# Four edits of order and place in a fused convolution and mixture-of-experts kernel: earlier first raw weights, a later softmax in the ramp, one ring for row blocks, another bank for a third tile

## The chip, the cores and the metric

One core of a Trainium2 chip runs the whole kernel. The metric is the device time of one execution in microseconds (us). The kernel before took 1184.83 us (median of three runs, 1182.57 to 1186.95). The execution that was profiled took 1184.11 us, of which 1182.5 us lie between its first and its last instruction; a trace covers that span.

Engines: PE multiplies matrices (PEld is its weight load), DVE and ACT work elementwise, POOL computes some and starts the scatters, SP only starts DMAs. Each runs its own instructions in order and waits on semaphores for the others.

## The reference

```python
# 1: causal convolution over 7 positions with a softmax of the given weights, per head
w = exp(weight_gen - max);  w = w / (sum(w) + 1e-9)            # (8, 2880, 8 heads, 7)
x_unf = x_pad[:, idx]                                          # 7 rows back, D = 192 = 8 heads x 24
out = einsum('bshk,bskhg->bshg', w, x_unf)
# 2: two-level routing of N = 23040 tokens: 4 groups x 4 experts, the best one of each
g_idx = argmax(x @ w_group);  e_idx = argmax(xg @ w_expert[g]) # top 1
h  = maximum(xg @ w1[g, e], 0.0)                               # 192 -> 1024
ye = h @ w2[g, e]                                              # 1024 -> 192
out[tok] = g_w * e_w * ye
```

## The kernel before

**Groups.** The tokens go through the first part in 15 groups of 12 slots x 128 partitions. For a group, `load_group` loads x and the weights `wt`; `softmax` works on `wt` (L268 to L282, DVE, with one exponential on ACT at L271); `conv` makes the seven products with x (L297) and adds them (L315) on DVE, for the first six half groups partly by PE matmuls with the identity (L338); `logits` transposes the result on PE (L395, L396) and multiplies by the routing weights; `ranks` finds each token's expert and its rank there, with two small matmuls (L462, L463) that need the one-hot matrix `oh` (L452). POOL then scatters the rows to DRAM by expert (L506).

**Blocks.** The second part works on blocks of rows of one expert. `ROUNDS` says which blocks may be taken after which group: a `table` made on DVE holds each block's place and expert. The order is 10 single blocks of 128 rows (blocks 0 to 9, "singles", `plain`), then blocks of two tiles (256 rows) from block 10 on, one block of three tiles (61), and in the last round blocks 77 to 86 of three tiles ("wide"; 80 to 86 cut), 87 and 88 of two, 89 to 92 of two cut ones, 93 and 94 single. A block takes 4 units (8 if wide); each unit is one `gemm1` (L939, into `ph`, ACT relu into `hh`) and, two units later, one `gemm2` (L977, or L979 and L980, into `py`). `finish` scales `py` by the gate on ACT (L986, for the later blocks with a DVE step L992) and `send` scatters `y` on POOL (L994).

**Inputs of a block.** `load(n, 0)` loads its rows `xb` (L804); `load(n, 1)` and `load(n, 2)` its first weights: two halves of `wa` straight for a single (L819), or for the others into `raw` buffers (L821, L828, the last piece from `w1lo`), which ACT casts to `wa` (L845, L854) with a DVE subtraction for the low part (L869). `load(n, 3)` loads the second weights (L832). All go through SP in the order in which `ask` and `pump` put them. `ask_x(n + 3)` follows `finish(n)`. In the unit u = 0 of a block, ACT copies the next block's columns (`prep_d`, L894); in u = 1 PE transposes its tiles (`prep_x`, L901 for a single, L912 and L913 into `tpx` otherwise), ACT copies them to `xh` (L919) and DVE makes `xl` (L869).

**Order.** The program is written by a planner: `clk` holds the modelled times of the engines, `fill` takes steps of the front part (`front`, `step`, `beside`) as long as DVE's modelled time is behind that of PE, and `after`, `delay` hold back DVE steps. So a changed cost or condition in one place can move steps elsewhere. `side` holds the next softmax, taken three steps at a time in `beside`.

**Buffers that the change touches.** `xb` stands in three tiles of four places, taken by `n % 3`; a two-tile block takes the half `n // 3 % 2`, a wide one the first three places. A load waits until the block that had those places has been scattered: six blocks back for two tiles, three back for wide ones. PSUM tile `tpx` (pool `ps_x`) has one buffer, and so has `tp` (pool `ps_t`), which the logits and the singles use.

Of the kernel before, what the change touches and what calls it, by code (L numbers as in the profile page):

```python
# [9 lines left out]
F32 = mybir.dt.float32  # L10
# [32 lines left out]
def conv_moe_kernel(ctx: ExitStack, tc: tile.TileContext, x, wgen, w_group, w_expert, w1, w2, out):  # L43
# [5 lines left out]
    P = 128  # L49
# [13 lines left out]
    W = D + 2  # L63
# [8 lines left out]
    ENDS = [r[0] for r in ROUNDS]  # L72
# [6 lines left out]
    FIRST = ENDS[0]  # L79
# [4 lines left out]
    tiles_of = lambda nb: CUT.get(nb, nb)  # L84
# [126 lines left out]
            return tiles[(at[0] if i is None else i) % n]  # L211
        return take

    xbs = [const.tile([P, 4, W], F32, name=f"xb{i}") for i in range(3)]
    new_ix = ring("ix", 3, [P, 1], I32)
    new_xd = ring("xd", 2, [P, 3, 2, HP])
    new_xh = ring("xh", 2, [P, 2, 3 * P], F32R)
# [440 lines left out]
    def front():  # L658
        side = []
        set_up()  # L660
        load_group(1)
        next(slow[0][0])
        yield from softmax(0, 0, SC)
        rest = softmax(0, SC)

        def pace(g):
            return 99 if g <= FIRST else HURRY if g < MAIN + 3 else 8 if g in ENDS else 2

        def beside(g, n):
            rush = g >= FIRST and not grp[FIRST - 1].routed  # L670
            if not rush:
                for q in list(slow):
                    yield from move(slow, q, 2)
            for q in side[:1]:
                if not rush:
                    yield from move(side, q, 3)
            yield from routing(g)

        def routing(g):
            if ranking:  # L680
                yield from move(ranking, ranking[0], pace(g))
            if scoring and (not ranking or g < FIRST):
                yield from move(scoring, scoring[0], pace(g) if scoring[0][2].chunks == 2 or g >= FIRST - 1 else 3)

        def settle(g):
            while not grp[g].routed:
                qs = ranking or scoring
                q = qs[0]
                yield from move(qs, q, 99)
                if qs and qs[0] is q and q[1] is not None:  # L690
                    yield Until(q[1][1]) if q[1][0] == "time" else NEXT

        for g in range(ENDS[-1]):
            o = grp[g]
            o.routed = False
            scoring.append([logits(g, o), None, o])
            for n, c in enumerate(conv(g, o)):
                yield c
                if g == 0 and n < 6:
                    for c in islice(rest, None if n == 5 else 1):  # L700
                        yield c
                if n == (2 if state["slots"] else 0) and 1 <= g < ENDS[-1] - 1:
                    load_group(g + 1)
                if n >= (12 if state["slots"] else 4) and not o.ahead and g + 1 < ENDS[-1] and g != FIRST - 1:
                    o.ahead = True
                    side.append([softmax(g + 1), None])
                yield from beside(g, n)
                if g == FIRST - 1 and n in (7, 8):
                    if n == 7:
                        soft = softmax(FIRST)  # L710
                    yield next(soft)
            if g == FIRST - 1:
                for n, c in enumerate(soft):
                    yield c
                    yield from beside(g, n)
            yield from finish_all(side)
            if g:
                yield from settle(g - 1)
        yield from settle(ENDS[-1] - 1)
# [49 lines left out]
    order = []  # L769
# [11 lines left out]
    def plain(n):  # L781
        return order[n][1] == 1

    def load(n, part):
# [11 lines left out]
        o = visits[n]  # L796
        if part == 0:
            nt = tiles_of(nb)
            h = 0 if nt == 3 else n // 3 % 2 * 2
            o.xb = xbs[n % 3][:, h:h + nt, :]  # L800
            o.tx = arrive[r, nb]
            rv = nc.sync.value_load(tab[q:q + 1, 0:1], min_val=0, max_val=NROW)
            full = nt - (nb in CUT)
# [89 lines left out]
        b.td = run("act", 0.1 + 0.13 * b.nt, b.o.tx)  # L893
        nc.scalar.copy(out=b.xd, in_=b.x[:, :, P:D].unsqueeze(2).broadcast_to([P, b.nt, 2, HP]))  # L894

    def prep_x(b, t0):
        fill(b.o.tx)
        if b.plain:
            tp = ps_t.tile([P, 3, P], F32, name="tp")
# [5 lines left out]
            b.txl = 0.0  # L905
            return
        m = min(2, b.nt - t0)
        tp = ps_x.tile([P, 2, 2, P], F32, name="tpx")[:, :, 0:m]
        tpv = tp.rearrange("p a t q -> p a (t q)")
        for t in reversed(range(m)):  # L910
            lo = max(0, min(t * P, b.n - (t0 + 1) * P))
# [109 lines left out]
    def blocks(n0, n1, paced):  # L1021
# [24 lines left out]
        def ask_w(n):  # L1046
            ask(n, 1)
            ask(n, 2)
# [66 lines left out]
        for i in range(len(units) + LAG):  # L1115
            if i < len(units):
                n, u = units[i]
                last = units_of(n) - 1
                gemm1(cur, u)
                queue.append((cur, u))  # L1120
                nxt_at = i + last + 1 - u
                if nxt_at < len(units):
                    if u == 0:
                        pump(units[nxt_at][0])
                        nxt = block(nxt_at)
                        prep_d(nxt)
                    if u == 1:
                        prep_x(nxt, 0)
                    if u == last // 2 + 1 and nxt.nt > 2:
                        prep_x(nxt, 2)  # L1130
                if u == last and i + 1 < len(units):
                    cur = nxt
            asks = []
# [7 lines left out]
            if i < len(units):  # L1141
                n, at = units[i]
                end = at == last
                if end and n + 3 < n1 and (plain(n + 3) or plain(n + 2)):
                    ask_w(n + 3)
                    if not plain(n + 3):
                        ask_w(n + 4)
                did = 0
                for job in list(jobs):
                    m, part, h = job  # L1150
# [60 lines left out]
```

## Time and profile before

| what | value |
|---|---|
| median of three runs | 1184.83 us |
| profiled execution, its own time | 1184.11 us |
| its span | 1182.5 us |
| PE busy | 1119.3 us (95%) |
| DVE busy | 957.2 us (81%) |
| ACT busy | 644.5 us (55%) |
| POOL busy | 572.4 us (48%) |
| granted PE clock, mean | 0.989 of full |
| DMA | 275.10 MB, mean 233 GB/s |

The first 113 us or so hold only the front part; singles run until about 205 us, two-tile blocks until about 955 us, wide ones until about 1105 us, and the rest to the end. The convolutions end near 870 us.

### The profile page before, as it was taken

The page shows a single profiled execution, that of the slowest core. Times are in us where ns is not written, and L with a number is a line of the kernel's source. Part 1 is how long each engine was busy: PE and PEld are TensorE (multiplying, and loading weights), DVE is VectorE, ACT ScalarE, POOL GpSimd, SP SyncE. Part 2 cuts the span into 40 slices and gives each one's busy share as a digit, 9 for nine tenths or more (in the row PEclk, how much of TensorE's full clock was granted, in tenths as well). Part 3 has the DMA queues.
Part 4 walks back from the last instruction along what each step waited for, and adds up shares of the span by engine and source line. Part 5 has one row for each costly group of instructions (what it writes and reads, how often), then busy time and mean ns, then how long its engine had stood idle before and what let it go on. Part 6 is the DMA issues. An engine that isn't in the chain of part 4 may idle for free. (4 is left out here: it accounts for less than half of the span.)

```text
span 1182.5 us, 24615 instructions
## 1 busy us (share of the span) xinstructions
PE 1119.3 (95%) x8357; PEld 1061.8 (90%) x8357; DVE 957.2 (81%) x1682; ACT 644.5 (55%) x1235; POOL 572.4 (48%) x613
## 2 busy tenths in 40 slices
PE   5787899999999999999999999999999989999998
PEld 2444789999999999999999999999899989999997
DVE  8899897999998999999999999998554756556661
ACT  1341334655556556556555556555556756666562
POOL 7164173847174756565555648373766112222211
PEclk9998999999999999999999999999999999999999
DMA  5798799786878886978787968667789774655562
GB/s 174 215 315 227 244 304 313 236 293 210 282 237 278 265 254 213 303 224 290 222 294 217 305 207 281 197 199 222 233 259 254 220 210 138 176 172 181 154 210 79
DMA packets 84520, 275.10 MB, mean 233 GB/s; under 512 B 15490, under 2 KB 34378, under 8 KB 82592
## 3 DMA queue, kind: packets, MB, share of 16 engines
q1 hardware_dynamic: 64056, 229.77, 62.4%
q0 software_dynamic: 20208, 43.39, 12.0%
q8 instruction: 67, 1.10, 0.4%
q14 instruction: 69, 0.57, 0.2%
q10 hardware_dynamic: 120, 0.28, 0.1%
HBM read 225.83 MB, written 48.42 MB: 232 GB/s over the span
## 5 line engine op out<-in xcount | busy, mean ns | idle before, releaser
L939 PE MATMUL ph<-xh,wa 128*128 128x256 f32 (+3 forms) x1992 | 454.3, 303 | 0.0
L994 POOL DMA_INDIRECT out<-y,xb x189 | 207.3, 1097 | 429.0 <-DVE y L992 186.5
L977 PE MATMUL py<-wc,hh 128*128 128x192 f32 x2160 | 400.3, 326 | 2.4 <-ACT y L986 2.4
L939 PE MATMUL ph<-xl,wa 128*128 128x256 f32 (+3 forms) x1328 | 351.4, 285 | 0.3 <-DVE xl L869 0.3
L977 PEld LDWEIGHTS py<-wc,hh 128*128 128x128 f32 x2160 | 346.3, 190 | 2.6 <-ACT y L986 2.6
L939 PEld LDWEIGHTS ph<-xh,wa 128*128 128x128 f32 x1992 | 336.7, 190 | 3.3 <-issue 1.8
L945 ACT ACTIVATE hh<-ph 128x512 f32<-128x512 f32 (+2 forms) x296 | 165.4, 559 | 260.9 <-PE ph L939 258.5
L297 DVE TENSOR_TENSOR pr<-xin,wt 128x1152 f32<-128x1152 f32 x186 | 249.1, 1352 | 3.9 <-PE py L338 3.5
L939 PEld LDWEIGHTS ph<-xl,wa 128*128 128x128 f32 x1328 | 251.6, 189 | 0.6 <-DVE xl L869 0.6
L506 POOL DMA_INDIRECT rows<-xrow,ix x156 | 224.5, 1439 | 48.1 <-POOL ix L505 35.0
L315 DVE TENSOR_TENSOR xrow<-xrow,pr 128x1152 f32<-128x1152 f32 x144 | 194.8, 1353 | 0.7
L869 DVE SCALAR_TENSOR_TENSOR pr<-ph,hh 128x320 fp32r<-128x320 f32 (+2 forms) x128 | 71.8, 561 | 99.9 <-ACT hh L950 99.3
L869 DVE TENSOR_TENSOR wa<-raw,wa 128x1024 fp32r<-128x1024 f32 x83 | 101.4, 1222 | 25.4 <-ACT wa L845 25.4
L979 PE MATMUL py<-wc,hh 128*128 128x384 f32 x352 | 111.7, 364 | 0.0
L505 POOL COPY ix<-posi 128x1 int32<-128x1 int32 x156 | 70.1, 459 | 68.4 <-DMA rows<-xrow,ix 41.9
L950 ACT ACTIVATE hh<-ph 128x320 fp32r<-128x320 f32 (+2 forms) x128 | 63.7, 498 | 65.9 <-PE ph L939 65.8
L845 ACT CAST wa<-raw 128x1024 fp32r<-128x1024 f32 x83 | 87.1, 1049 | 3.4 <-DMA raw<-in_moe_w 3.4
L980 PE MATMUL py<-wc,pr 128*128 128x192 f32 x352 | 88.4, 251 | 0.0
L854 ACT CAST wa<-raw 128x1024 fp32r<-128x1024 f32 x83 | 86.7, 1045 | 0.0
L986 ACT ACTIVATE y<-py,xb 128x192 f32<-128x192 f32 x179 | 67.1, 422 | 22.2 <-PE py L977 20.2
L869 DVE TENSOR_TENSOR xl<-tpx,xh 128x512 fp32r<-128x512 f32 (+2 forms) x94 | 60.1, 640 | 14.6 <-ACT xh L919 14.1
L979 PEld LDWEIGHTS py<-wc,hh 128*128 128x128 f32 x352 | 66.5, 189 | 1.4
(188 smaller groups left out, 1352.4 us busy)
## 6 DMA issues: line engine op xcount, KB each, us to landing
wc<-in_moe_w SPq DMA_DIRECT2D x73, 768.0 KB
raw<-in_moe_w SPq DMA_DIRECT2D x83, 512.0 KB
xin<-in_x SPq DMA_DIRECT2D x14, 1728.0 KB
raw<-in_moe_w SPq DMA_DIRECT2D x91, 256.0 KB
raw<-w1lo SPq DMA_DIRECT2D x83, 256.0 KB
raw<-in_moe_w SPq DMA_DIRECT2D x22, 768.0 KB
xb<-rows SPq DMA_DIRECT2D x75, 194.0 KB
wa<-in_moe_w SPq DMA_DIRECT2D x24, 384.0 KB
```

Of the source, the lines that this page charges most:

```text
L297: nc.vector.tensor_tensor(out=dst, in0=o.xin[:, c0 + k:c0 + k + SC, :].rearrange("p s (h g) -> p s h g", g=HG), in1=w4[:, c0:c0 + SC, :, k ...
L315: nc.vector.tensor_tensor(out=acc, in0=acc, in1=prs[k - 2], op=ALU.add)
L506: written_once(nc.gpsimd.indirect_dma_start(out=rows[:, :], out_offset=bass.IndirectOffsetOnAxis(ap=ix, axis=0), in_=src, in_offset=None, ...
L845: nc.scalar.copy(out=o.wa[:, 0, :], in_=o.raw[0])
L854: nc.scalar.copy(out=o.wa[:, 2, :], in_=o.raw[1])
L869: f(*a, **k)
L939: nc.tensor.matmul(ph[:, v, :], lhsT=w[:, f0:f0 + P], rhs=rhs, start=i == 0, stop=i == len(terms) - 1)
L945: nc.scalar.activation(out=hh, in_=ph, func=AF.Relu)
L977: nc.tensor.matmul(b.acc[t], lhsT=hh[:, v, c], rhs=wc[0][:, f, :], start=f == 0 and not (b.wide and t == 1), stop=f == NFT - 1 and not (b. ...
L979: nc.tensor.matmul(b.py[t], lhsT=hh[:, v, c], rhs=wc[f // 4][:, f % 4].rearrange("p l d -> p (l d)"), start=f == 0, stop=False)
L980: nc.tensor.matmul(b.acc[t], lhsT=hl[:, v, c], rhs=wc[f // 4][:, f % 4, 0, :], start=False, stop=f == NFT - 1)
L994: ins = nc.gpsimd.indirect_dma_start(out=out[:, :], out_offset=bass.IndirectOffsetOnAxis(ap=b.x.bitcast(I32)[:, t, D + 1:D + 2], axis=0), ...
```

## The change

Line numbers of the rows of the changed program are 10 higher from L224 on, because of the new lines above.

1. **First raw weights.** At the end of single n with n + 3 the last single and n + 4 the first larger block, the larger block's first weights (`ask_w(n + 4)`) are asked for, and ahead of the single's. Before, they were asked for one block later, together with those of the block behind. The block behind (11) is still asked for there.
2. **Softmax in the ramp.** While the blocks of two tiles have not begun (`state["slots"]` is false), the next group's softmax is put into `side` behind the 12th step of the convolution, no longer behind the 4th; not for the groups up to `FIRST` (2).
3. **Row blocks as one ring.** One tile of 12 places; each block takes the next two (or three) places, and the ring starts over where a block would not fit. Two-tile blocks meet the places of the sixth block back as before (the fifth in blocks 62 to 69); wide ones those of the fourth back (the fifth for blocks 77 and 78), where it was the third; block 89 those of block 84, where it was 86.
4. **Other bank for a third tile.** Where the block that runs is not wide and the next one is (blocks 61 and 77), the third tile is transposed in the same unit as the first two (u = 1), into `tp`; before it was in u = 2, into `tpx`, which the first two tiles fill in u = 1.

```diff
-    xbs = [const.tile([P, 4, W], F32, name=f"xb{i}") for i in range(3)]
+    NXB = 12
+    xbs = const.tile([P, NXB, W], F32, name="xb")
+    places = []
+
+    def place(n):
+        while len(places) <= n:
+            at = sum(places[-1]) if places else 0
+            nt = max(2, tiles_of(order[len(places)][1]))
+            places.append((at if at + nt <= NXB else 0, nt))
+        return places[n][0]
...
-                if n >= (12 if state["slots"] else 4) and not o.ahead and g + 1 < ENDS[-1] and g != FIRST - 1:
+                if n >= (12 if state["slots"] or g > FIRST else 4) and not o.ahead and g + 1 < ENDS[-1] and g != FIRST - 1:
...
-            h = 0 if nt == 3 else n // 3 % 2 * 2
-            o.xb = xbs[n % 3][:, h:h + nt, :]
+            h = place(n)
+            o.xb = xbs[:, h:h + nt, :]
...
-        tp = ps_x.tile([P, 2, 2, P], F32, name="tpx")[:, :, 0:m]
+        tp = ps_t.tile([P, 2, 1, P], F32, name="tp") if beside else ps_x.tile([P, 2, 2, P], F32, name="tpx")[:, :, 0:m]
...
-                    if u == last // 2 + 1 and nxt.nt > 2:
-                        prep_x(nxt, 2)
+                    if nxt.nt > 2 and u == (last // 2 + 1 if cur.wide else 1):
+                        prep_x(nxt, 2, not cur.wide)
...
-                if end and n + 3 < n1 and (plain(n + 3) or plain(n + 2)):
+                if end and n + 4 < n1 and plain(n + 3) and not plain(n + 4):
+                    ask_w(n + 4)
                     ask_w(n + 3)
-                    if not plain(n + 3):
-                        ask_w(n + 4)
+                elif end and n + 3 < n1 and plain(n + 3):
+                    ask_w(n + 3)
+                elif end and n + 4 < n1 and plain(n + 2):
+                    ask_w(n + 4)
```

The planner turns the second edit into another order on DVE. The place is the convolution of group 3 in the ramp; `wt_1071` is the weight tile of group 4, `mxg` the first step of the ranking of group 2. Before:

```order
L297 TENSOR_TENSOR pr_1082<-xin_702,wt_700 128x1152
L268 TENSOR_REDUCE m_1084<-wt_1071 128x96
L270 TENSOR_TENSOR wt_1071<-wt_1071,m_1084 128x672
L315 TENSOR_TENSOR xrow_1057<-xrow_1057,pr_1079 128x6x192
L297 TENSOR_TENSOR pr_1089<-xin_702,wt_700 128x1152
L315 TENSOR_TENSOR xrow_1057<-xrow_1057,pr_1082 128x6x192
```

In the changed program, at the same place (`pr_1080` is what `pr_1082` was):

```order
L307 TENSOR_TENSOR pr_1080<-xin_700,wt_698 128x1152
L325 TENSOR_TENSOR xrow_1055<-xrow_1055,pr_1077 128x6x192
L307 TENSOR_TENSOR pr_1083<-xin_700,wt_698 128x1152
L325 TENSOR_TENSOR xrow_1055<-xrow_1055,pr_1080 128x6x192
L307 TENSOR_TENSOR pr_1086<-xin_700,wt_698 128x1152
L325 TENSOR_TENSOR xrow_1055<-xrow_1055,pr_1083 128x6x192
```

The two first softmax steps of group 4 have gone from between the convolution steps; they and one addition stand now behind the ranking's `ohe` and ahead of `ohs` and `oh`. The three steps on `z` stood between the convolution and `mxg` and come now behind `oh`, and a product and an addition stand ahead of `mxg` in their place. The same happens once more, in the convolution of group 4 with the softmax of group 5.

SP's queue at the end of single 6, before (`xb2_177` and `wc_1758` are those of block 8, `wa_1791` is that of block 9, `raw00` and `raw10` are those of block 10):

```order
L832 DMA wc_1758<-in_moe_w2 128x1536
L816 TENSOR_LOAD tab1_820
...
L819 DMA wa_1791<-in_moe_w1 96x1024
...
L804 DMA xb0_175<-rows_89 128x194
...
L832 DMA wc_1843<-in_moe_w2 128x1536
L816 TENSOR_LOAD tab2_1374
...
L821 DMA raw00_195<-in_moe_w1 128x1024
```

And in the changed program:

```order
L842 DMA wc_1753<-in_moe_w2 128x1536
L826 TENSOR_LOAD tab2_1394
...
L831 DMA raw00_193<-in_moe_w1 128x1024
...
L838 DMA raw10_195<-in_moe_w1 64x1024
...
L838 DMA raw10_195<-w1lo_90 64x1024
L826 TENSOR_LOAD tab1_818
...
L829 DMA wa_1800<-in_moe_w1 96x1024
```

The three raw loads of block 10 now stand directly behind a `wc` load and ahead of the `wa` loads of block 9, which they followed.

PE in unit 2 of block 76, whose next block is the wide block 77 (`hh` and `pr` here are relu's high and low part). Before, behind the gemm1 of the unit, stand the third tile's two transposes and then the gemm2:

```order
L912 MATMUL tpx<-ident,xb_177 128x128
L913 MATMUL tpx<-ident,xd_181 128x128
L979 MATMUL py_13019<-wc,hh 128x384
L980 MATMUL py_13019<-wc,pr 128x192
L979 MATMUL py_13020<-wc,hh 128x384
```

In the changed program they stand in unit 1, directly behind those of the first two tiles, and go into `tp`; from the second tile's on:

```order
L922 MATMUL tpx<-ident,xb 128x128
L923 MATMUL tpx<-ident,xd_179 128x128
L922 MATMUL tp<-ident,xb 128x128
L923 MATMUL tp<-ident,xd_179 128x128
L989 MATMUL py_12872<-wc,hh 128x384
```

So no transposes stand between gemm1 and gemm2 of unit 2 any more.

## Rows read from the trace of the kernel before

**Rows 1.** the page: its span, and section 1.

```profile
span 1182.5 us, 24615 instructions
...
PE 1119.3 (95%) x8357; PEld 1061.8 (90%) x8357; DVE 957.2 (81%) x1682; ACT 644.5 (55%) x1235; POOL 572.4 (48%) x613
```

**Rows 2.** 270:300: length, busy PE PEld DVE ACT POOL, clock, DMA share, GB/s.

```profile
270.00:300.00 30.00, 30.00 (x223) 29.94 (x224) 29.96 (x27) 16.66 (x31) 18.66 (x17) 1.00 0.76 247
```

**Rows 3.** who PE waited for: us in total, times, longest us.

```profile
PE pl L462 <- DVE oh L452: 4.6, 2, 3.0
...
PE py L977 <- ACT y L986: 2.4, 1, 2.4
...
PE tpx L912 <- DVE xl L869: 4.8, 7, 3.7
```

**Rows 4.** four stretches of 3.4 us, same columns.

```profile
139.70:143.10 3.40, 3.40 (x15) 3.37 (x15) 3.33 (x12) 0.73 (x2) 0.00 (x0) 0.50 0.30 121
...
173.90:177.30 3.40, 2.82 (x49) 2.37 (x44) 3.37 (x4) 0.48 (x1) 0.82 (x2) 0.50 1.00 414
...
194.30:197.70 3.40, 3.40 (x14) 3.40 (x15) 3.19 (x15) 1.27 (x3) 1.39 (x4) 0.51 1.03 318
...
955.50:958.90 3.40, 3.40 (x17) 3.40 (x17) 0.00 (x0) 0.83 (x2) 0.00 (x0) 0.50 0.63 162
```

**Rows 5.** PE in time order: start, length, work, idle before, releaser.

```profile
139.68 0.31 PE L462 MATMUL pl<-oh,tri 128*128 128x192 bf16 x1 [3.02 <-DVE oh L452]
```

**Rows 6.** DVE in order of time, 119 to 140.

```profile
119.12 1.35 DVE L297 TENSOR_TENSOR pr<-xin,wt 128x1152 f32<-128x1152 f32 x1
...
124.06 0.85 DVE L268 TENSOR_REDUCE m<-wt 128x96 f32<-128x672 f32 x1 [3.59 <-DMA wt<-in_weight_gen]
...
125.72 1.35 DVE L315 TENSOR_TENSOR xrow<-xrow,pr 128x1152 f32<-128x1152 f32 x1
...
132.06 0.85 DVE L276 TENSOR_REDUCE z<-wt 128x96 f32<-128x672 f32 x1
...
133.86 0.14 DVE L349 TENSOR_REDUCE mxg<-ls 128x12 f32<-128x48 f32 x1
...
138.27 0.85 DVE L282 TENSOR_TENSOR wt<-wt,z 128x672 f32<-128x672 f32 x1
...
139.27 0.36 DVE L452 TENSOR_TENSOR oh<-ohg,ohs 128x192 bf16<-128x192 f32 x1
```

**Rows 7.** ACT in order of time near 192.

```profile
192.28 1.04 ACT L845 CAST wa<-raw 128x1024 fp32r<-128x1024 f32 x1 [3.43 <-DMA raw<-in_moe_w]
```

**Rows 8.** SP's DMA starts in order of time, 170 to 184.

```profile
170.09 0.87 SPq L832 DMA_DIRECT2D wc<-in_moe_w  x1
...
180.17 0.86 SPq L819 DMA_DIRECT2D wa<-in_moe_w  x2
...
183.57 0.33 SPq L821 DMA_DIRECT2D raw<-in_moe_w  x1
```

**Rows 9.** stretch 170 to 176, columns as in group 2.

```profile
170.00:176.00 6.00, 4.50 (x59) 3.77 (x61) 3.43 (x5) 2.80 (x7) 3.08 (x4) 0.82 1.03 362
```

**Rows 10.** PE in order of time near 951.

```profile
950.84 0.28 PE L939 MATMUL ph<-xl,wa 128*128 128x256 f32 x1
...
954.78 0.30 PE L912 MATMUL tpx<-ident,xb 128*128 128x128 f32 x1 [3.67 <-DVE xl L869]
```

**Rows 11.** DVE in order of time near 954.

```profile
953.95 0.68 DVE L869 TENSOR_TENSOR xl<-tpx,xh 128x512 fp32r<-128x512 f32 x1
```

**Rows 12.** PE in order of time near 1117.

```profile
1116.90 0.33 PE L912 MATMUL tpx<-ident,xb 128*128 128x128 f32 x1 [1.51 <-DMA xb<-rows]
```

**Rows 13.** who SP waited for between 1098 and 1116.

```profile
SPq L804 <- DMA out<-y,xb: 19.9, 2, 10.4
```

**Rows 14.** DVE near 440: the one-hot matrix of a later ranking.

```profile
440.46 0.36 DVE L452 TENSOR_TENSOR oh<-ohg,ohs 128x192 bf16<-128x192 f32 x1
```

**Rows 15.** PE near 447: the matmul that reads it.

```profile
447.39 0.25 PE L462 MATMUL pl<-oh,tri 128*128 128x192 bf16 x1
```

More of the change, by code (lines that the diff above doesn't have):

```diff
@@ L894, in prep_d, with prep_x @@
         nc.scalar.copy(out=b.xd, in_=b.x[:, :, P:D].unsqueeze(2).broadcast_to([P, b.nt, 2, HP]))
-    def prep_x(b, t0):
+    def prep_x(b, t0, beside=False):
         fill(b.o.tx)
```

## The prediction

> **What bounds the kernel now.** Read the page first: PE is busy for 1119.3 of 1182.5 us [rows 1], so the most that any edit of order can give back is the 63 us in which PE is idle, plus what PE loses to its slow clock. Then the table by stretches. From about 215 to 780 us PE is busy throughout; in the stretch 270 to 300 it reads 30.00 of 30, with DVE at 29.96 [rows 2]. Nothing is to be had there, and DVE has nothing to spare. Third, the list of PE's waits: three long ones stand in it, 3.0, 2.4 and 3.7 us [rows 3], near 139, 194 and 954 us; a fourth, of 1.51, ends at 1116.90 [rows 12]. Each lies where one of the four edits works. Last, the clock: in four stretches of about 3.4 us PE's granted clock reads 0.50 or 0.51, the 1.2 GHz level of the two, and three of the four follow directly on the first three waits [rows 4]. At half the clock 3.4 us hold 1.7 us of work, so each such stretch costs 1.7 us wherever PE has work all through it. A wait is thus dearer than its own length.
>
> The sum is made against the profiled execution's own 1184.1 us (span 1182.5 and 1.6 around it); the median of the runs is 0.7 above that.
>
> **The softmax in the ramp.** At 139.68 PE starts a matmul that waited 3.02 us for the one-hot matrix; PE was free at 136.66 [rows 5]. DVE was late because it stood 3.59 us before the first softmax step of group 4, whose weights had not landed, and then did that step and the next (124.06 to 125.72, 1.66 us), three steps on z (132.06 to 133.86, 1.80) and one product by z (138.27 to 139.0, about 0.76) before the matrix at 139.27 [rows 6]. The changed order has eight convolution steps from 119.12 to the ranking's first step. Five such steps take 125.72 to 132.06, so one takes 1.27, and the ranking begins at 129.3 and not at 133.86. From there to the matrix it was 5.41; the product by z leaves, the first two softmax steps come in, a convolution step stands on both sides: 5.41 - 0.76 + 1.66 = 6.3. The matrix starts at 135.6 and is there at 136.0, 0.7 before PE asks for it. What is late next is PE itself. I take the whole 3.0 and the slow stretch, 1.7 [rows 4]: **4.7**. From below it is 0, if DVE meets another wait of 3 us there; from above 4.7. The steps on z now stand behind the matrix, in front of what follows in the ranking; 3.6 us of head start cover their 1.8. The moved weights' load is not moved against its use except to the good side: it had landed by 124.06 and is now first read near 134.
>
> **The first raw weights.** ACT starts the first cast at 192.28 after a wait of 3.43 us for the raw load [rows 7]; in ACT's queue behind it stand a relu, a copy and the scaling of a finished block, and PE waited 2.4 us for that scaling, since it needs the bank [rows 3]. SP started that load at 183.57, so it took 8.7 us to land. But SP had been free since 171.0, when the start of a `wc` load ended; it stood in front of the single's `wa` loads, whose buffer PE freed only at 180.17 [rows 8]. The edit puts the raw loads ahead of that waiting instruction, so they start near 171, 12.5 us earlier, and even at 8.7 us to land they are there at 179.7, 9 us before ACT asks (192.28 - 3.43 = 188.85). PE's wait of 2.4 and the slow stretch behind it, 1.7, go: **4.1**, with 0 below. The cost: 1 MB (two tiles of 128 x 1024 numbers of 4 bytes) now stands in the queue before the single's weights. The stretch 170 to 176 shows all DMA engines in use and 362 GB/s [rows 9], at which 1 MB takes 2.9 us. The single's weights still start at 180.17, held by PE; the raw loads have 9 us until then, so I take nothing for it. Later, block 11's loads follow in their old place.
>
> The Trainium skill ("DMA: Bandwidth & Descriptors", section "Queues, rings and completion order") says that each DMA engine takes a queue's descriptors in ring order. By that rule what is asked ahead delays what is asked behind by its whole length; taken in full, block 9 would wait 2.9 us and meet a slow stretch of its own, and this edit would give 4.1 - 4.6 = -0.5. The row agrees that the engines are full, but not that the single's weights are near them in the queue.
>
> **Third tile.** At 954.78 PE starts the third tile of block 77 after 3.67 us for the `xl` that frees `tpx`; the last matmul before it ends at 951.1 [rows 10]. DVE makes that `xl` from 953.95 to 954.63 [rows 11]. With another bank the transposes need nothing but data that the first two tiles have too, so the 3.67 and the 1.7 behind go. What is late next is the first use of block 77's `xl`: DVE writes the third tile's part directly behind the first, 0.68 at most, so until 955.3. Were it needed at 951.1, a wait of 4.2 would take the old one's place and the gain would be 0 or a little below. But three more runs of matmuls (a gemm2, a gemm1, a gemm2) stand between, so I take 0.3 for it: 3.7 + 1.7 - 0.3 = **5.1**. Block 61 has no such wait in the list, so it gives nothing.
>
> **One ring.** PE waited 1.51 us before 1116.90 for the rows of block 89 [rows 12]. In that neighbourhood SP stood 19.9 us in two waits for scatters [rows 13], because a load had to see the block three places back leave. Now block 89 meets block 84, long gone; its load starts some us earlier and the 1.5 go: **1.5**, between 0 and 1.5. The other wide blocks' loads start earlier too, but nobody on PE waited for them. Elsewhere two-tile blocks keep a distance of five or six, and their loads are asked for three ahead; I take nothing.
>
> **What is given back.** From 200 us on PE runs 8.8 us ahead of its old times. DVE gains about as much from the waits that it loses (3.59 at the first place, [rows 6], and less at the second), but its margin is thin around 270 [rows 2], and the second moved softmax now falls into the first two-tile blocks. The nearest row for DVE against PE is a ranking where the matrix is ready at 440.82 and read at 447.39, 6.6 us later [rows 14, 15]; no wait of PE for DVE is listed there. Between 0 and the whole 8.8 I take **1.0** lost, near the lower end for that margin.
>
> Sum: 4.7 + 4.1 + 5.1 + 1.5 - 1.0 = 14.4; 1184.1 - 14.4 = 1169.7, and with the 0.7 to the median 1170.
>
> **Rivals.**
> 1. The waits go and the slow stretches stay, or move. For it: the slow stretch at 173.9 follows on no long wait; in the 6 us from 170 PE still reads 4.50 busy [rows 9], so short gaps are enough for it. Against it: the other three follow on waits of 2.4 us and more. Three times 1.7 comes back: 1170.3 + 5.1 = 1175. The Trainium skill ("TensorE: Matmul & The Clock Gate", Part 1) has the slow state as the default, which activity releases; the trace's 0.50 and 1.00 are its two states, and it leaves open which of these gaps were enough.
> 2. The ramp's gain is given back: DVE at 29.96 of 30 is the real bound until 300, and PE waits for it as it comes closer. The 8.8 shrink to 0 in place of 1.0: 1170.3 + 7.8 = 1178. Against it the margin of 6.6 [rows 14, 15].
> 3. The edit to the asking order doesn't do what it says, since SP stops at the raw loads for a buffer or for `w1lo`: 1170.3 + 4.1 = 1174. Against it: these buffers have no earlier block in them.
> 4. Slower: the planner, reckoning with a DVE that is ahead, puts the ranking's matmul one or two units earlier on PE in each of ten rounds. If DVE lags by more than the 6.6 us of margin less those units (about 2 us a unit), PE waits in every round, about 1 us, and is sent to half clock each time: 10 x (1.0 + 1.7) = 27 us, 1170.3 + 27 = 1197. It decides from a lag of some 3 to 4 us on; I see about none.
>
> **How the numbers follow.** Forecast 0.58, rival 1 0.14, rival 2 0.12, rival 3 0.09, rival 4 0.07. Own range of the forecast 1166 to 1174. About 0.5% (6 us) is what a measurement can tell from no change, so faster means below 1178.9. The forecast, rivals 1 and 3 and a part of rival 2 are faster: 0.58 + 0.14 + 0.09 + 0.02 = 0.83, less 0.02 for what I have not seen: 0.81. The same: 0.12, most of it rival 2. Slower: 0.07. The range runs from 1165, all four terms whole and a slow stretch less, to 1179, rival 2's end.
>
> **What would show it.** In the changed profile: no wait of PE for `oh` near 136 and none for the scaling near 190; ACT's first cast waits for no load; PE's first two-tile block begins 8 to 9 us earlier (it began near 204); no wait at the third tile, and half clock neither there nor in the ramp behind those places; no wait for `xb` near 1100. Wrong would be any of: new waits of PE for DVE between 200 and 300, the half-clock stretches at shifted places, or a wait for block 9's `wa`.

## The result, and the profile after

The changed kernel took 1175.49 us (median of 6 runs, 1173.67 to 1178.71), the kernel before in the same series 1185.82 (6 runs). The ratio is 0.9902, 95% interval 0.9883 to 0.9921: 10.3 us or 1.0% faster. The forecast was 1170, its own range 1166 to 1174, the full range 1165 to 1179. So the sign is right and the time lies in the full range, though outside the forecast's own. 4 of the 14.4 us of the sum are missing, and they are not missing evenly: the two edits at the end gave more than their terms, the two in the ramp 1.5 to 2.6 us together in place of 7.8.

The page after, its span and section 1, against [rows 1]:

```profile
span 1172.4 us, 24606 instructions
PE 1113.9 (95%) x8357; PEld 1057.7 (90%) x8357; DVE 954.8 (81%) x1682; ACT 644.6 (55%) x1235; POOL 576.4 (49%) x613
```

This execution took 1174.01 us as a whole, the one before 1184.11, with PE's instructions the same in number. Whom PE waited for after (us in total, times, longest), against [rows 3]:

```profile
PE tp L406 <- ACT rem L398: 5.8, 5, 2.2
PE pl L406 <- ACT rem L398: 3.6, 4, 1.6
PE tp L911 <- DMA xb<-rows: 2.8, 1, 2.8
PE pl L472 <- DVE oh L462: 1.6, 1, 1.6
```

The waits of 3.0, 2.4 and 3.7 us of [rows 3] are gone (the 1.6 left for `oh` lies before 90 us). But a wait for a single's rows (`xb`) has come in, and one of 2.2 for ACT's `rem`. The 1.6 for `rem` at 231.58 is not new: the kernel before has a wait of the same 1.64 at 269.09. Another for `rem`, of 0.88 at 265.83, is. The places, PE in order of time, the idle time before an instruction and its releaser in brackets:

```profile
137.13 0.25 PE L472 MATMUL pl<-oh,tri 128*128 128x192 bf16 x1
...
187.60 0.66 PE L911 MATMUL tp<-ident,xb 128*96 128x128 f32 x2 [2.84 <-DMA xb<-rows]
...
207.63 0.33 PE L406 MATMUL tp<-ident,rem 128*128 128x128 f32 x1 [2.17 <-ACT rem L398]
...
231.58 0.33 PE L406 MATMUL pl<-ident,rem 128*128 128x128 f32 x1 [1.64 <-ACT rem L398]
...
947.06 0.27 PE L922 MATMUL tp<-ident,xb 128*128 128x128 f32 x1
...
1107.74 0.27 PE L922 MATMUL tpx<-ident,xb 128*128 128x128 f32 x1
```

The first row answers to [rows 5], the last two to [rows 10] and [rows 12]: no brackets, no wait. Two stretches after (length, busy time of PE, PEld, DVE, ACT, POOL, granted clock, DMA share, GB/s), against [rows 4]:

```profile
186.70:193.60 6.90, 6.00 (x25) 5.99 (x26) 4.98 (x25) 2.10 (x4) 4.30 (x6) 0.51 0.99 305
...
949.00:956.00 7.00, 7.00 (x52) 6.88 (x51) 5.71 (x10) 5.28 (x9) 1.94 (x2) 1.00 0.78 264
```

Half clock (0.51, the 1.2 GHz level) now follows on the new wait for `xb`, for twice as long as before at 194; at the third tile and near 140 and 174 it is gone (near 140 and 174 it is missing in one later trace too in which the order there is the old one, see "Edits alone").

Where the time went is best read from the start of the same block in both traces (the first transposes of its rows). The number is the changed kernel's start less that of before, in us:

| place | before | after | offset |
|---|---|---|---|
| block 2 | 130.75 | 131.62 | +0.87 |
| block 8 | 183.07 | 177.77 | -5.30 |
| block 9 | 189.47 | 187.60 | -1.87 |
| block 10 | 200.62 | 196.86 | -3.76 |
| block 12 | 218.88 | 217.47 | -1.41 |
| block 22 | 334.08 | 333.43 | -0.65 |
| block 77 | 948.07 | 946.62 | -1.45 |
| block 78 | 963.44 | 955.95 | -7.49 |
| block 88 | 1105.71 | 1098.23 | -7.48 |
| block 89 | 1116.90 | 1107.74 | -9.16 |
| block 93 | 1155.72 | 1145.63 | -10.09 |

Up to block 2 PE does the same in both programs, so the first 0.87 is put down to this execution. The ramp then gains 6.2 by block 8 (4.7 were forecast up to there; most of the rest is the half-clock stretch near 174 that is missing) and loses 4.7 of it again by block 22. The third tile is worth 6.0, the ring 2.6.

### The profile page after: what moved, and what is told of

It reads as the page before. It is cut to its first block, busy times and chain, and to the rows that moved or that the text cites. A ratio compares the mean times of both kernels' runs of the same rounds, so it can differ in the third digit from the quotient of the medians.

```text
span 1172.4 us, 24606 instructions
## 1 busy us (share of the span) xinstructions
PE 1113.9 (95%) x8357; PEld 1057.7 (90%) x8357; DVE 954.8 (81%) x1682; ACT 644.6 (55%) x1235; POOL 576.4 (49%) x613
## 5 line engine op out<-in xcount | busy, mean ns | idle before, releaser
L1004 POOL DMA_INDIRECT out<-y,xb x189 | 219.9, 1164 | 413.5 <-DVE y L1002 177.8
L516 POOL DMA_INDIRECT rows<-xrow,ix x156 | 218.5, 1401 | 47.8 <-POOL ix L515 35.1
L879 DVE TENSOR_TENSOR xl<-tpx,xh 128x512 fp32r<-128x512 f32 (+1 forms) x92 | 59.3, 645 | 18.9 <-ACT xh L929 18.6
```

Source lines behind the costliest of these rows:

```text
L516: written_once(nc.gpsimd.indirect_dma_start(out=rows[:, :], out_offset=bass.IndirectOffsetOnAxis(ap=ix, axis=0), in_=src, in_offset=None, ...
L879: f(*a, **k)
L1004: ins = nc.gpsimd.indirect_dma_start(out=out[:, :], out_offset=bass.IndirectOffsetOnAxis(ap=b.x.bitcast(I32)[:, t, D + 1:D + 2], axis=0), ...
```

## What the new waits hang on

At 184.22 SP starts the load of block 9's rows, 2.3 us later than before (181.89), though PE runs 5 us ahead. It stood 7.7 us for a scatter, whose rows the load overwrites (single 3 had the places of single 9, before as now). First the changed kernel: SP's waits between 165 and 200.

```profile
SPq L814 <- DMA out<-y,xb: 7.7, 1, 7.7
```

That scatter on POOL and the load's start on SP, in order of time:

```profile
176.55 0.97 POOL L1004 DMA_INDIRECT out<-y,xb  x1 [0.30 <-issue]
...
184.22 0.35 SPq L814 DMA_DIRECT2D xb<-rows  x1
```

And the stretch between them (columns as above):

```profile
176.50:184.20 7.70, 7.70 (x61) 7.50 (x60) 5.61 (x14) 3.69 (x10) 5.40 (x4) 1.00 1.00 285
```

The kernel before at the same place, the scatter, the load, and the stretch around them:

```profile
179.30 0.97 POOL L994 DMA_INDIRECT out<-y,xb  x1 [0.30 <-ACT hh L945]
...
181.89 0.35 SPq L804 DMA_DIRECT2D xb<-rows  x1
```

```profile
178.00:182.00 4.00, 4.00 (x33) 4.00 (x32) 3.11 (x10) 1.68 (x5) 3.09 (x4) 1.00 0.71 257
```

Before, the scatter was done at most 2.6 us after its start, on engines in use for 0.71 of the time; after, 7.7 us, on engines in use all the time, since the raw weights now come there first. That is theory A: the raw weights asked ahead delay the scatter, the scatter the rows, the rows PE. Full engines alone are not the whole of it. In the run below with group 4's later softmax alone, which asks for the raw weights in the old order, the same scatter took at most 5.1 us (175.11 to the load's start at 180.18) on engines as full:

```profile
175.11:180.18 5.07, 5.07 (x41) 5.07 (x41) 4.79 (x12) 1.59 (x5) 2.91 (x3) 1.00 1.02 355
```

The second new wait is that for `rem` at 207.63. DVE after in order of time:

```profile
190.74 1.35 DVE L325 TENSOR_TENSOR xrow<-xrow,pr 128x1152 f32<-128x1152 f32 x1
...
197.23 1.23 DVE L879 TENSOR_TENSOR wa<-raw,wa 128x1024 fp32r<-128x1024 f32 x1 [5.14 <-ACT wa L855]
...
198.97 0.84 DVE L278 TENSOR_REDUCE m<-wt 128x96 f32<-128x672 f32 x1
...
200.63 1.35 DVE L307 TENSOR_TENSOR xrow<-xin,wt 128x1152 f32<-128x1152 f32 x1
...
204.98 0.85 DVE L286 TENSOR_REDUCE z<-wt 128x96 f32<-128x672 f32 x1 [0.47 <-ACT wt L281]
...
206.78 1.29 DVE L325 TENSOR_TENSOR xrow<-xrow,pr 128x1152 f32<-128x1152 f32 x1
```

Five steps of group 5's softmax, about 3.5 us, stand here between steps of the convolution; the second edit moved them from 174. Theory D of the runs below says that they make `rem`, and so PE, late. The rival is that DVE is late only because it stood idle for 5.1 us behind block 9 (theory A again), or that DVE bounds this stretch whatever is done (theory B).

That the moved softmax is the cause will hold; the way by DVE does not, and this trace already shows it. ACT's copy `rem` starts at 207.04, while the addition of 206.78 runs until 208.07, so that addition did not release it. It belongs to the next half group, whose first product is the row at 200.63; the half that `rem` copies was summed by the addition of 190.74, and PE read it at 205.08 without a wait. What `rem` stands behind is ACT's own queue, busy without a pause from 202.45 on, with group 5's exponential (204.19) in it:

```profile
202.45 0.60 ACT L955 ACTIVATE hh<-ph 128x512 f32<-128x512 f32 x1 [1.42 <-PE ph L949]
...
204.19 0.76 ACT L281 ACTIVATE wt<-wt 128x672 f32<-128x672 f32 x1
...
207.04 0.54 ACT L398 COPY rem<-xrow 128x384 f32<-128x384 f32 x1
```

And PE comes for `rem` early: its transposes follow directly on the gemm2 of the unit in which it transposes block 11's rows, with no further unit between.

```profile
204.43 0.82 PE L987 MATMUL py<-wc,hh 128*128 128x192 f32 x4
205.08 0.38 PE L405 MATMUL tp<-ident,xrow 128*128 128x128 f32 x2
```

## Experiments

The first four ran on a chip on which the kernel before took 1223.5 us (17 runs, 1219.0 to 1235.1) and PE stood idle in front of its own matmuls, most of all in the product with the routing weights, for nothing that the profile shows ("issue"; here PE's waits in the changed kernel with the old softmax threshold):

```profile
PE pl L388 <- issue: 11.1, 19, 1.1
```

Ratios there carry intervals of 0.35 to 0.5% to either side; these runs serve for their traces above all, and "the first chip" below means this one. The other eight ran where the kernel before took 1186.69 and 1185.96.

**Rows of singles 6 to 9 in unused places** (odd places of the ring, so their loads need no scatter to be over; no instruction moves).

```diff
-            h = place(n)
+            h = place(n) + (r == 0 and n > 5)
```

> 

> The changed kernel, with the rows of singles 6 to 9 put into the odd places of the ring (1, 3, 5, 7), which no block has used; so their loads wait for no scatter. Nothing else moves. Theory A (the raw weights asked ahead fill the DMA engines, the scatter of block 3 lands 7.6 us after its issue and not 2.6, and SP's load of block 9's rows stands behind it until 184.2; PE then waits 2.8 us and is at half clock for 6.8, and DVE idles 5.1 behind it): PE has no wait for xb near 187, no half clock from 186 to 194, DVE's idle of 5.1 before its wa step falls under 2, block 10 begins at 191 to 193 in place of 196.9, and the kernel takes 1169 to 1172 us against 1175.5 of the changed one. Theory B (DVE bounds from 200 us on and the ramp's gain is lost in any case): the wait for xb goes, but PE's waits for ACT's rem near 207 and 231 grow from 2.2 and 1.6 to 5 or more together with others, and the time stays at 1174 to 1177.

Ratio 0.9853 (0.9807 to 0.9900) on the first chip. PE still waited 1.2 us for the rows, and 2.8 for `rem` at 207. Theory A in its full form had promised no wait. Again, beside the unaltered changed kernel on one chip:

> 

> The changed kernel, unaltered, as the yardstick for the others of this call: 0.988 to 0.993 of the kernel before. In its trace the new waits should stand again: PE for block 9's rows near 187 (about 2.8 us), PE for ACT's rem near 207 (about 2.2) and near 231 (about 1.6).

> 

> Singles 6 to 9 in the odd places of the ring, beside the changed kernel on the same chip. Theory A (the wait of the load for the scatter is what costs): 4 to 6 us below the changed kernel. Theory C (the row load stands behind 1 MB of raw weights in its own queue as well, and DVE's second moved softmax makes PE wait near 207 in any case): PE still waits about 1.2 us for block 9's rows, and the time is within 2 us of the changed kernel.

The changed kernel 1176.91 (ratio 0.9914, 0.9892 to 0.9937); with the odd places 1176.28 (0.9904, 0.9880 to 0.9929): the same. SP and then PE with the odd places, in order of time:

```profile
177.00 0.87 SPq L829 DMA_DIRECT2D wa<-in_moe_w  x2
178.66 0.35 SPq L814 DMA_DIRECT2D xb<-rows  x1
```

```profile
187.50 0.42 PE L911 MATMUL tp<-ident,xb 128*96 128x128 f32 x2 [0.61 <-DMA xb<-rows]
...
206.49 0.33 PE L406 MATMUL tp<-ident,rem 128*128 128x128 f32 x1 [2.64 <-ACT rem L398]
```

The load no longer waits for the scatter, it starts 5.6 us earlier than in the changed kernel's first trace, and PE still finds its rows only at 187.5, 8.8 us after. The Trainium skill ("DMA: Bandwidth & Descriptors", "Queues, rings and completion order"), weighed in the prediction, has each engine take one queue's descriptors in ring order; these rows fit that, with 1 MB of raw weights (169.39 to 171.1) and the 0.8 MB of `wa` (from 177.00) asked for ahead in the same queue. They don't prove it: the engines were in use all the time from 169.39 to 187.50, which by itself would delay the rows too. And where the wait for the rows shrinks to 0.6, that for `rem` takes over (2.64). The unaltered kernel had, in this second trace, 1.3 us for the rows and 2.8 for `rem`. All three traces reach block 14 within 0.3 us of each other (244.66, 244.48, 244.78): a shorter wait for the rows is made up for by a longer one at `rem`. Theory A names a true wait, but taking it away gains nothing; it came out as theory C had it.

**Group 5's softmax back at four steps**, group 4's left late.

```diff
-                if n >= (12 if state["slots"] or g > FIRST else 4) and not o.ahead and g + 1 < ENDS[-1] and g != FIRST - 1:
+                if n >= (12 if state["slots"] or g == FIRST + 1 else 4) and not o.ahead and g + 1 < ENDS[-1] and g != FIRST - 1:
```

> 

> The changed kernel with the later softmax for group 4 alone; group 5's softmax is back at four steps. Theory D (the second moved softmax, 3.5 us of DVE between two convolution steps at 199 to 206, is what makes PE wait 2.2 us for ACT's rem near 207 and again near 231): both waits fall under 0.5 us, the wait for oh near 139 stays away, and the time is 2 to 4 us below the changed kernel, unless DVE now stands for group 5's weights before 174, as it did in the kernel before (2.5 us). Rival (DVE is late near 207 because of its 5.1 us of idle behind block 9's rows): the wait near 207 stays at 2 us or more, and the time is the same within 1.5 us.

1173.23 us (0.9883, 0.9858 to 0.9909), 3.7 below the changed kernel; the two intervals overlap a little, but four of the six runs lie below the lowest of the changed kernel's six (1175.44). DVE near 170, and below it whom PE waited for:

```profile
170.22 0.85 DVE L278 TENSOR_REDUCE m<-wt 128x96 f32<-128x672 f32 x1 [2.50 <-DMA wt<-in_weight_gen]
```

```profile
PE tp L406 <- ACT rem L398: 4.4, 4, 1.6
PE tp L911 <- DMA xb<-rows: 3.0, 1, 3.0
```

The wait of 2.2 for `rem` is gone (5.8 in 5 waits became 4.4 in 4). That of 1.6 at 231.58 is gone from there, but the same 1.64 now stands at 263.09, as at 269.09 in the kernel before. Block 12 begins 5.9 us ahead of the kernel before, block 22 still 6.3. (This trace is of the fastest of the six executions, 1168.72.) DVE stands 2.5 us for group 5's weights, as the kernel before did, and that costs PE nothing. The rival falls by DVE's idle time at block 10: 1.73 here and 1.96 in the second trace of the changed kernel, almost the same, and only the latter has the wait. First this run, then the changed kernel, DVE and PE:

```profile
195.12 1.23 DVE L879 TENSOR_TENSOR wa<-raw,wa 128x1024 fp32r<-128x1024 f32 x1 [1.73 <-DMA wc<-in_moe_w]
```

```profile
195.25 1.23 DVE L879 TENSOR_TENSOR wa<-raw,wa 128x1024 fp32r<-128x1024 f32 x1 [1.96 <-ACT wa L855]
...
205.88 0.33 PE L406 MATMUL tp<-ident,rem 128*128 128x128 f32 x1 [2.81 <-ACT rem L398]
```

So theory D holds in what it blames, the second moved softmax, and theory B is out. How it acts is shown by PE's order here:

```profile
202.31 0.82 PE L987 MATMUL py<-wc,hh 128*128 128x192 f32 x4
...
204.12 1.46 PE L987 MATMUL py<-wc,hh 128*128 128x192 f32 x8
...
206.60 1.46 PE L987 MATMUL py<-wc,hh 128*128 128x192 f32 x8
...
208.12 0.27 PE L406 MATMUL tp<-ident,rem 128*128 128x128 f32 x1
```

Two units (each a gemm1 and a gemm2) now stand between block 11's transposes and those of `rem`, as in the kernel before. ACT starts `rem` at 207.35, no earlier than the 207.04 of the changed kernel, and PE does not wait, since it comes later itself. With both softmaxes late the planner puts these transposes two units earlier on PE, ahead of what ACT can deliver.

**Both: odd places, and group 5's softmax at ten steps.**

```diff
-            h = place(n)
+            h = place(n) + (r == 0 and n > 5)
-                if n >= (12 if state["slots"] or g > FIRST else 4) and not o.ahead and g + 1 < ENDS[-1] and g != FIRST - 1:
+                if n >= (12 if state["slots"] or g == FIRST + 1 else 10 if g > FIRST else 4) and not o.ahead and g + 1 < ENDS[-1] and g != FIRST - 1:
```

> 

> The odd places and group 5's softmax at ten steps in place of twelve, so that its first two steps stand ahead of the ranking's last part and the other three directly behind block 10's xl. If both theories hold (the load's wait and the second softmax's place), PE's wait near 207 falls under 1 us and the time is 4 to 7 us below the changed kernel; if DVE bounds the stretch from 200 to 300 in any case, within 2 us of it.

1170.92 us (0.9861, 0.9836 to 0.9886), 6.0 below the changed kernel, and its interval lies wholly below that kernel's. PE's waits for `rem` are those of the run before. One unit stands between block 11's transposes and those of `rem`, and group 5's last softmax steps come before 200:

```profile
203.07 1.57 PE L987 MATMUL py<-wc,hh 128*128 128x192 f32 x8
...
204.90 0.33 PE L406 MATMUL tp<-ident,rem 128*128 128x128 f32 x1
```

This is the fastest version measured. Its interval overlaps that of the run before, and ten steps without the odd places was not run, so what each of the two adds is open.

**Edits alone, and the rest without one.** First the order of asking alone, the kernel before with that hunk of the change and nothing else:

```diff
-                if end and n + 3 < n1 and (plain(n + 3) or plain(n + 2)):
+                if end and n + 4 < n1 and plain(n + 3) and not plain(n + 4):
+                    ask_w(n + 4)
                     ask_w(n + 3)
-                    if not plain(n + 3):
-                        ask_w(n + 4)
+                elif end and n + 3 < n1 and plain(n + 3):
+                    ask_w(n + 3)
+                elif end and n + 4 < n1 and plain(n + 2):
+                    ask_w(n + 4)
```

> 

> The kernel before with the new order of asking for weights alone. Prediction's term 4.1 (2.4 of PE's wait for the scaling and a slow stretch of 1.7): ratio 0.9965, 1182.6 where the kernel before takes 1186.7. Theory E (what stands behind the raw weights in the queue and on the DMA engines pays: block 9's rows come later, so that PE waits for them): 0 to 2 us, ratio 0.998 to 1.000.

1185.48 (0.9993, 0.9973 to 1.0012). The prediction's 0.9965 is outside. ACT no longer waits for the raw load, but SP stands 7.1 us for the scatter and PE 2.4 for block 9's rows, at half clock behind it, which is theory E. SP's wait, PE in order of time, and the stretch:

```profile
SPq L804 <- DMA out<-y,xb: 7.1, 1, 7.1
```

```profile
190.22 0.63 PE L901 MATMUL tp<-ident,xb 128*96 128x128 f32 x2 [2.43 <-DMA xb<-rows]
```

```profile
190.00:194.00 4.00, 3.78 (x17) 3.58 (x18) 1.68 (x7) 1.72 (x3) 0.97 (x1) 0.57 1.02 350
```

This trace also shows how far half clock differs between executions. PE waits 2.49 us for `oh` at 140.59, as the kernel before waits 3.02, and near 172 it has the same short gaps (0.69, 0.24 and 0.57), but at neither place does the clock fall. Instead it falls at 268.8, behind the 1.64 for `rem` (266.95) behind which the kernel before stays at full clock:

```profile
139.70:143.10 3.40, 2.51 (x19) 2.37 (x19) 3.37 (x13) 0.76 (x3) 0.00 (x0) 1.00 0.83 271
173.90:177.30 3.40, 2.80 (x48) 2.53 (x37) 2.73 (x3) 1.82 (x4) 1.20 (x2) 1.00 1.00 404
268.80:272.20 3.40, 3.40 (x15) 3.40 (x14) 3.40 (x5) 0.71 (x2) 3.12 (x4) 0.50 0.29 67
```

Group 4's later softmax alone, on the kernel before:

```diff
-                if n >= (12 if state["slots"] else 4) and not o.ahead and g + 1 < ENDS[-1] and g != FIRST - 1:
+                if n >= (12 if state["slots"] or g == FIRST + 1 else 4) and not o.ahead and g + 1 < ENDS[-1] and g != FIRST - 1:
```

> 

> The kernel before with the later softmax for group 4 alone. Prediction's term 4.7 in the ramp; if it holds to the end, ratio 0.996. Theory F (the raw loads, still asked behind the single's weights, can't come earlier with PE, so that PE's wait for the scaling near 190 grows from 2.4 to about 6.5, as it stood in the changed kernel with the old order of asking): all of it but 1 us is lost at that place, ratio 0.999 or more.

1185.23 (0.9991, 0.9972 to 1.0009). The wait for `oh` is gone, and the wait for the scaling has grown from 2.4 to 3.4, with a longer half-clock stretch behind it (ACT's and PE's rows, and the stretch):

```profile
189.85 1.04 ACT L845 CAST wa<-raw 128x1024 fp32r<-128x1024 f32 x1 [4.39 <-DMA raw<-w1lo]
...
191.80 1.65 PE L977 MATMUL py<-wc,hh 128*128 128x192 f32 x4 [3.37 <-ACT y L986]
```

```profile
190.00:198.00 8.00, 6.20 (x25) 6.20 (x26) 6.21 (x28) 3.46 (x7) 3.38 (x7) 0.60 1.02 272
```

Theory F has the direction right, but the size in its text (6.5, from a trace of the first chip) is too much.

The changed kernel with group 5 at four steps (the diff above), and the hunk of edit 1 taken back:

> 

> The changed kernel with group 5's softmax back at four steps and the old order of asking; against the run with the same softmax and the new order (0.9883 of the kernel before) it prices that order. Theory F: PE waits 6 us or more for the scaling, the gain of the ramp is gone by block 12, ratio 0.992 to 0.994 (the tail's gain alone). Theory E: the order is worth little, ratio 0.988 to 0.990.

1174.52 (0.9915, 0.9896 to 0.9933): between the two theories, and its interval touches both. PE waits 3.4 us for the scaling. Against the run with group 5 alone put back, the order of asking is worth 0.3% of time, but over two series and with overlapping intervals.

The changed kernel with the hunks of edits 1 and 2 taken back, so that the ring and the third tile's bank alone are left:

> 

> The kernel before with the one ring and the other bank for the third tile; both edits of the ramp are left out. By the prediction's terms 5.1 + 1.5 = 6.6 us, ratio 0.9944. By the offsets of the blocks between the two traces 6.0 at the third tile and 2.6 where the ring works, 8.6, ratio 0.9927; then nearly all of the changed kernel's gain (0.990 to 0.991) is the tail's, and the ramp's two edits together give 1 to 2 us.

1175.92 (0.9933, 0.9912 to 0.9955): 8 us by the ratio, 10.0 by the medians of the series (1185.96 before). By this, some 8 of the changed kernel's 10 us are the tail's; 0.9944, the prediction's terms, is inside the interval too, so the time alone does not tell 6.6 from 8.6. The offsets do: from block 77 to block 93 this trace gains 8.6, 6.0 of them at the third tile.

Last the three others of the first chip. The changed kernel with the hunk of edit 1 taken back:

> 

> The changed kernel with the old order of asking for weights (a single's own wa ahead of the first raw loads). By the prediction's term for the first raw weights (4.1 us gained) this takes 1179 to 1180. Theory A (the edit pays for the wait it removes with the new wait for block 9's rows): block 9's rows are in time (no xb wait), PE waits again about 2.4 us for the scaling and meets one half-clock stretch of 3.4, and the time is 1174 to 1177, the same as the changed kernel within its interval.

0.9874 (0.9827 to 0.9922) on the first chip. No wait for block 9's rows is listed, and PE waited 6.5 us for the scaling, where 2.4 were expected.

The changed kernel with edit 2 taken back (`if n >= (12 if state["slots"] else 4)`):

> 

> The changed kernel with the old threshold of four steps for the next softmax in the ramp. Prediction's term: PE waits 3 us for oh near 140 and a half-clock stretch follows, so single 8 begins 4.7 us later than at 177.8; if all of that reached the end, 1179 to 1181. Theory B (the ramp's gain is lost again by 240 us because DVE and the loads bound there): at most 1 us of it reaches the end, 1175 to 1177.

0.9881 (0.9845 to 0.9916) on the first chip; the changed kernel did not run there, so that no time decides. The trace has no wait for `rem` near 207, as theory D wants; the longest is the 1.64, at 271.59.

The kernel before with the two hunks of edit 4 (`beside` in `prep_x`, and its call in unit 1):

> 

> The kernel before with the other bank for the third tile alone. Prediction's term 5.1: the wait of 3.7 for xl at 954 and the half clock behind it go, 1180 to 1181 us. What the comparison of the two traces gives there is 6.0 (offsets of the blocks at 948 and 963 us), so 1179 to 1181. Rival (the next wait, for the third tile's xl, takes its place): 1184 to 1186.

0.9961 (0.9926 to 0.9995) on the first chip, 4.8 us of 1223.5; the expected 0.995 is inside. The wait for `xl` is gone.

To set the ramp's parts side by side, the offset against the kernel before at block 22 less that at block 2, which takes out what differs between executions before the edits begin. What differs behind block 2 stays in: each row is one execution, and a half-clock stretch more or less moves it by some 1.7 us.

| kernel | block 2 | block 22 | ramp |
|---|---|---|---|
| changed (two traces) | +0.87, +1.77 | -0.65, -0.83 | -1.5, -2.6 |
| odd places | +3.00 | -0.53 | -3.5 |
| group 5 at four steps | -0.16 | -6.27 | -6.1 |
| the same, old asking | +1.25 | -3.64 | -4.9 |
| odd places, ten steps | +0.38 | -6.84 | -7.2 |
| asking alone | +1.69 | -0.51 | -2.2 |
| group 4's softmax alone | +2.79 | +0.61 | -2.2 |
| tail alone | +1.65 | +1.49 | -0.2 |

So the -2.2 of asking alone is not that edit's. Between blocks 8 and 10, where it works, the trace gains 0.2 us; the rest are the two half-clock stretches that are missing near 140 and 174, a shorter wait for `oh`, and the stretch near 269 that came in. A difference in this column counts where the times bear it out, as the 3.5 to 4.6 us between the changed kernel and group 5 at four steps (3.7 by time).

## Why the prediction was right in sign and off in size

**The softmax in the ramp, 4.7.** Right at its place: the matrix was there when PE asked at 137.1, block 4 begins 4.9 us earlier counted from block 2, and the slow stretch is gone. Of the 4.7 the 3.0 of the wait are the edit's; the 1.7 are not sure to be, since with the old softmax that stretch came in one trace and not in another (asking alone). The term looked at one of the two softmaxes that the edit moves.

**What is given back, 1.0.** This step failed. The prediction did say that the second moved softmax falls into the first two-tile blocks, and priced it by a margin of 6.6 us between a one-hot matrix and its matmul at 440 [rows 14, 15]. That is another dependence at another time, and DVE's margin was not what counted. The second moved softmax changed the planner's order: PE comes for `rem` two units earlier than before, and `rem` stands in ACT's queue. That cost waits of 2.17 and 0.88 us (2.81 and 0.88 in the second trace, with a half-clock stretch behind the first). The run with group 5 alone put back gives 3.7 us of time, and 3.5 to 4.6 of offset, where 1.0 was allowed.

**The first raw weights, 4.1.** Failed in the sentence "I take nothing for it". The wait of 2.4 and the 1.7 behind it went, and 2.84 for block 9's rows with 6.9 us at half clock (PE busy for 6.0 of them, so some 3 us of work lost) came. The prediction looked at the single's `wa`; what was late is the row load behind it, by way of a scatter in another queue, and, where that wait is taken away, still behind what was asked ahead of it. The prediction had worked out almost this, a wait of 2.9 for block 9 with a slow stretch and -0.5 in all, and set it aside because the weights were not near in the queue. Alone, the edit is worth 0.8 us (-1.4 to 3.2) and not 4.1; once the softmax is right it may be worth more, 1.2 by the offsets of two single traces.

**Third tile, 5.1.** Right, and a little small: 6.0, and the same 6.0 in every trace of a kernel with both edits of the end (alone, on the first chip, 4.3). The 0.3 for a late `xl` was not paid, and 0.6 more came in on the way to block 78.

**One ring, 1.5.** Right in kind, too small: 1.7 at block 89, 0.4 and 0.6 at blocks 90 and 91, 2.6 in all. The ring was never run alone, but no trace without it has this gain. The bound from above was too low, since only the listed wait was counted.

**The rivals.** Rival 2 (the ramp's gain shrinks to 0, 1178) describes the ramp well: 1.5 to 2.6 of 7.8 are left; but the cause is where steps stand in the order, not DVE's share of busy time. Rival 1 happened in part: one slow stretch, twice as long, in a new place. Its argument that short gaps are enough for the stretch near 174 holds for one trace: with the same gaps the clock stayed up in another. Rival 3 did not: the raw loads did start 15 us earlier (168.09 against 183.57 in [rows 8]). Rival 4 did not as it stands: no wait for `oh` in any ranking after 90 us, and nothing that comes in every round. But its mechanism, the planner putting PE's part earlier than it can be served, did, at the logits of two groups and for `rem`. That the forecast lay within 6 us is in part luck: 2.0 us that it did not see in the tail stood against some 6 that it lost in the ramp.

## What to carry to other kernels

When an edit moves a rule and not an instruction, list every instance that moves, and price each at the row where it lands, in the order of every engine that it changes: here one softmax gained 5 us and its twin gave 4 of them back, over PE's order and ACT's queue and not over DVE, where it runs. Before an instruction is called the cause of a wait, see that it ends before the waiting one starts. When a load is asked for earlier, follow all that stand behind it on the DMA engines, scatters and what waits for them too, and not only the next load in the queue. And a wait that is taken away is worth only the distance to the next one: counting block by block against the old trace shows where that is, sooner than totals do, as long as half-clock stretches that differ by execution are counted apart.

## What the runs showed of the hardware

A scatter that landed within 2.6 us of its start with the DMA engines at 0.71 took 5.1 with them at 1.02, and 7.7 with them at 1.00 and 1 MB of weights asked for ahead. Half clock lasted about 3.4 us, about 6.9 or not at all behind waits of much the same length: 3.4 behind 2.41 before and behind 3.02 with group 5 alone put back, 6.9 behind 2.84 in the changed kernel, none behind 2.49 with the asking alone. And one chip of those used ran the kernel before 3% slower; in a changed kernel's trace there PE was idle before its own instructions, 11.1 us in 19 waits at one line; why, the profile does not show.
